# A fused attention, dense and expert kernel: the gather buffer is cleared earlier, `xe` is placed anew, idle products stand in the last routing

## The chip, the cores and the metric

The kernel runs on one core of one Trainium2 chip. The metric is the device time of one execution in microseconds (us). The engines are TensorE (PE in the profile, its weight loads PEld), VectorE (DVE), ScalarE (ACT), GpSimd (POOL) and SyncE (SP, which here only issues DMAs).

## The reference

Three layers follow one another on 1536 tokens (2 batches of 768) of width 512. Shown is the part in which the change lies:

```python
x = attention(q, k, v, lam)                  # linear attention with decay, (1536, 512)
x = (x @ w_a) * (x @ w_b) @ w_out            # dense layer, inner width 1536, float64 weights
# expert layer: 8 experts, 512 -> 1024 -> 512
do_compute = x @ w_skip > 0                  # the other tokens pass through unchanged
logits = xc @ w_gate                         # xc = x[do_compute]
e_idx = np.argmax(logits, axis=1)
gate_w = max(softmax(logits))
y[mask] = gate_w * (relu(xc[mask] @ w1[e]) @ w2[e])     # mask: e_idx == e
out[do_compute] = xc + y
```

## The kernel before

Products of float32 accuracy are made of three products each (`mm3`, line 418): every operand is kept as a high part, written by a ScalarE cast to fp32r, and a low part, the rest, written by VectorE (`lo_part`, line 50). So each stationary or moving operand costs one cast on ScalarE and one subtraction on VectorE before TensorE can use it.

The program goes through these stages, with their places in the profiled execution. Attention (up to 56 us) leaves `xT`. The dense stage (56 to 258 us) runs `phase_a(m, c)` 36 times, 24 products each, and writes the products `a * b` as `g`; SyncE meanwhile loads the next float64 weights, which `conv` turns into `ab` and `wo`. The y stage (258 to 372 us) goes over 12 token tiles of 128 rows: `y_tile(t)` multiplies `g` by `wo` in 12 steps `m` of three products (operands `gs`, from `y_split`), and at each step lets the routing of the tile before go on by one `yield`. That routing, `route`, has the following parts. `logits3` transposes y, cuts it into three bf16 parts `yp` and multiplies them by the gate weights `w9p` (line 605, twelve short products). Then VectorE takes the row maximum `mx`, the index `r`, the one-hot `oh`. `rank` multiplies `oh` by an upper triangle to number the tokens of each expert (`rk`, `rks`), forms the row `key`, and GpSimd scatters the rows of y into the buffer `xs` in DRAM, 128 rows for each of the 8 experts (`place`). Rows of `xs` which nobody writes must read as zero with token number 4096: `clear` writes a zero tile `blank` over all of `xs` at the start of the y stage, by eight SyncE DMAs.

The last tile (11) has a routing of its own, since nothing is left to cover it. Its y is made in two halves of 256 columns, the logits in two halves too (`logits`, lines 577 to 583). Expert 0's rows are not fetched from `xs` as a whole: `px_add` (line 686) adds three products in PSUM, one for `xg0` (the rows placed before tile 10) and two with one-hot matrices `pm` for tiles 10 and 11. From there ScalarE and VectorE make `xe0`.

The expert stage (376 to 477 us) has for each expert: `exp_x` (four transposes `px` of the gathered rows `xg`, then `xe`), `exp_h` twice (12 products `eu,xe` each, then ScalarE's relu into `hr`), `exp_t` (eight transposes of `hr`, then `hT`), and `exp_y` (24 products `eu,hT`, then the gated sum and an indirect DMA to `out`, whose row numbers `ix` are cast from a column of `xg`). The weights `eu` come through six raw buffers `rw` that SyncE fills; `prefetch` says how far ahead loads and casts are written, `load_pair` holds both. At the end stands a loop for tokens beyond 128 in an expert, which is not entered here; its count `npi` comes from `cnt`, `mxc`, `over` and `npf`.

Up to line 463 the order on every engine is that of the code. Behind it a scheduler decides the order on each engine, and each engine works its own queue strictly in order (TensorE can load weights ahead). DMA issues of SyncE also stand in a queue and wait in it for their buffers.

Of the kernel before, what the change touches and what calls it, by code (L numbers as in the profile page):

```python
# [17 lines left out]
P = 128  # L18
# [5 lines left out]
def kernel(ctx, tc, q, k, v, lam, w_a, w_b, w_out, w_skip, w_gate, w1, w2, out):  # L24
# [73 lines left out]
    spin(24)  # L98

# [319 lines left out]

    def phase_a(m, c, work):  # L420
# [12 lines left out]
        for i in range(2):  # L433
            nc.vector.tensor_mul(g[c * 2 + i][m // 4][:, m % 4, :], at[:, i * 256:(i + 1) * 256], pp[1][:, i * 256:(i + 1) * 256])  # L434
# [8 lines left out]
    for m, c in seq:  # L443
        if c == 0 and m + 1 < MT:
            lds, nxt_ab = load_ab(m + 1)
            lds[0]()
            if m < 8 and m % 2 == 0:
                nxt_wo = load_wout(m, W // 2)

        def work():  # L450
            if m == MT - 2:
                steps(nxt_ab, 4 if c == 0 else 0)
            elif m < MT - 2:
                steps(nxt_ab, 2 if c < 2 else 0)
                if c == 2 and m < 8:
                    steps(nxt_wo, 4)
            if (m, c) == (MT - 1, 1):
                steps(load_wout(8), 4)
            if (m, c) == (MT - 2, 2):
                steps(load_wout(10), 4)  # L460

        phase_a(m, c, work)
    msched.close()
# [8 lines left out]
    def load_pair(e, which, j, steady=True):  # L472
        rt = raw.tile([P, 2, W], F32, name=f"rw_{e}_{which}_{j}", tag="raw")
        if which == 0:
            nc.sync.dma_start(out=rt.rearrange("p a b -> p (a b)"), in_=w1[e, j * P:(j + 1) * P, :])
        else:
            nc.sync.dma_start(out=rt, in_=w2[e, j * 2 * P:(j + 1) * 2 * P, :].rearrange("(m p) d -> p m d", p=P))
        n = uno[0]
# [23 lines left out]
    def prefetch(upto):  # L502
        while nxt[0] < min(upto, len(useq)):
            eu[useq[nxt[0]]] = load_pair(*useq[nxt[0]])
            nxt[0] += 1
# [15 lines left out]
    xs = dp.tile([E * P, XW], F32, name="xs")  # L521

    def clear(blank):
        nc.gpsimd.memset(blank[:, :DM + 1], 0.0)  # L524
        nc.gpsimd.memset(blank[:, DM + 1:], 4096.0)
        for e in range(E):
            nc.sync.dma_start(out=xs[e * P:(e + 1) * P, :], in_=blank)

    clear(wk.tile([P, XW], F32, name="blank", tag="y", bufs=3))
# [12 lines left out]
    def y_tile(t, hooks):  # L542
# [3 lines left out]
        nc.gpsimd.iota(yt[:, DM + 1:DM + 2], [[0, 1]], base=t * P, channel_multiplier=1, allow_small_or_imprecise_dtypes=True)  # L546
        for half in range(2 if last else 1):
# [13 lines left out]
            nc.scalar.copy(out=yt[:, cols], in_=py)  # L561
# [8 lines left out]
    def logits(t, yt, lg, k0, k1):  # L570
# [4 lines left out]
        pt = bank([P, n, P], f"yT_{t}_{k0}")  # L575
        for kk in range(k0, k1):
            nc.tensor.transpose(pt[:, kk - k0, :], yt[:, kk * P:(kk + 1) * P], ident)
        yT = wk.tile([P, n, P], F32, name=f"yTs_{t}_{k0}", tag="yT")
        nc.vector.tensor_copy(yT, pt)
# [7 lines left out]
    def logits3(t, yt, lg):  # L587
# [12 lines left out]
        for _ in range(6):  # L600
            yield
# [8 lines left out]
    def route(t, yt, lg=None):  # L610
# [3 lines left out]
        if last:  # L614
            yield from logits(t, yt, lg, 2, KT)
# [14 lines left out]
        nc.vector.reduce_max(out=r, in_=cand, axis=AX)  # L630
        ina = sm("ina", 1)
        nc.vector.tensor_scalar(out=ina, in0=act, scalar1=-FAR, scalar2=FAR + E * P, op0=ALU.mult, op1=ALU.add)
        oh = sm("oh", E, BF16)
        nc.vector.tensor_scalar(out=oh, in0=cand, scalar1=r, scalar2=act, op0=ALU.is_equal, op1=ALU.mult)
# [12 lines left out]
    def rank(t, yt, oh, es):  # L647
# [6 lines left out]
        nc.tensor.matmul(rk, lhsT=upper, rhs=oh, start=(t == 0), stop=True)  # L654
        jk = sm("jk", E)
# [50 lines left out]
    def exp_x(e, xg):  # L706
# [3 lines left out]
        xe = wk.tile([P, 2, KT, P], F32R, name=f"xe_{e}", tag="xe")  # L710
# [60 lines left out]
    prefetch(17)  # L771
    do_h(0)
# [10 lines left out]
    hTs[0] = exp_t(0, hrs[0])  # L783
    for e in range(E):
        prefetch(8 * e + 14)

# [21 lines left out]
    passes = nc.values_load(npi[0:1, 0:1], min_val=0, max_val=NT1 - 1)  # L808
    with tc.For_i(0, passes):
# [10 lines left out]
        for t in range(NT1):  # L820
# [3 lines left out]
            nc.gpsimd.iota(yt[:, DM + 1:], [[0, 1]], base=t * P, channel_multiplier=1, allow_small_or_imprecise_dtypes=True)  # L824
# [33 lines left out]
```

## Time and profile before

| | us |
|---|---|
| three runs | 488.21, 490.44, 491.65 |
| median | 490.44 |
| profiled execution | 488.71 |
| its span in the trace | 486.9 |
| TensorE busy | 467.7 (96%) |
| VectorE busy | 367.8 (76%) |
| ScalarE busy | 219.5 (45%) |

Times in the rows further down count from the start of the span; a row of a timeline joins neighbouring instructions of one kind (its count behind the x) and gives the start of the first and the time to the end of the last. Ends of products are modelled, and products overlap, so a pace is read from starts. In brackets stands the idle time of the engine before the row, and what ended it.

### The profile page before, as it was taken

How to read it: one execution, taken by the hardware profiler on the slowest of the kernel's cores; microseconds unless marked ns; L12 is line 12 of the kernel's file. 1: busy time of each engine (PE TensorE's matmuls, PEld its weight loads, DVE VectorE, ACT ScalarE, POOL GpSimd, SP SyncE). 2: the span in 40 equal slices, each digit the busy share in tenths (PEclk: the TensorE clock that was granted, in tenths of full speed). 3: DMA queues.
4: the chain of work that ended last, by engine and by line, in shares of the span. 5: the costliest groups of instructions: out<-in, count | busy, mean ns of one | idle time of the engine just before them, and what ended most of it. 6: DMA issues, size and time to landing. Idle time of an engine off the chain costs nothing. (4 is left out here: it accounts for less than half of the span.)

```text
span 486.9 us, 7861 instructions
## 1 busy us (share of the span) xinstructions
PE 467.7 (96%) x2874; PEld 386.9 (79%) x2874; DVE 367.8 (76%) x740; ACT 219.5 (45%) x380; POOL 57.9 (12%) x84
## 2 busy tenths in 40 slices
PE   8999899999999999999999899999998999999991
PEld 6788788888888888888888678887788788888881
DVE  6568988888888888675495797776676579899880
ACT  3244333233323332222132754654553569877760
POOL 3544000000000000000000141121122000101000
PEclk9999999999999999999999999999999999999998
DMA  9999531421322314311207950110114898999941
GB/s 174 217 218 217 132 123 51 174 86 50 124 86 87 127 46 149 112 39 47 87 0 191 366 180 34 51 51 36 47 51 144 301 375 290 347 343 365 322 147 41
DMA packets 71629, 73.41 MB, mean 151 GB/s; under 512 B 41510, under 2 KB 53798, under 8 KB 71584
## 3 DMA queue, kind: packets, MB, share of 16 engines
q1 hardware_dynamic: 68880, 66.37, 43.7%
q0 software_dynamic: 2560, 6.47, 3.5%
q8 instruction: 24, 0.39, 0.3%
q14 instruction: 21, 0.17, 0.1%
q10 hardware_dynamic: 144, 0.00, 0.0%
HBM read 64.26 MB, written 10.51 MB: 154 GB/s over the span
## 5 line engine op out<-in xcount | busy, mean ns | idle before, releaser
L418 PE MATMUL psum<-xT,ab 128*128 128x512 f32 x864 | 196.1, 389 | 0.0
L418 PEld LDWEIGHTS psum<-xT,ab 128*128 128x128 f32 x864 | 162.1, 188 | 33.8 <-issue 0.2
L418 PE MATMUL psum<-wo,gs 128*128 128x512 f32 (+1 forms) x468 | 105.4, 378 | 0.0
L418 PEld LDWEIGHTS psum<-wo,gs 128*128 128x128 f32 x468 | 82.0, 188 | 14.6
L50 DVE TENSOR_TENSOR eu<-rw,eu 128x512 fp32r<-128x512 f32 (+1 forms) x92 | 78.5, 896 | 13.2 <-ACT eu L487 8.1
L434 DVE TENSOR_TENSOR g<-at,psum 128x256 f32<-128x256 f32 x72 | 27.0, 418 | 35.5 <-PE psum L418 35.5
L432 ACT COPY at<-psum 128x512 f32<-128x512 f32 x36 | 21.0, 585 | 61.0 <-PE psum L418 57.2
L418 PE MATMUL psum<-eu,xe 128*128 128x512 f32 x192 | 47.7, 405 | 0.0
L418 PE MATMUL psum<-eu,hT 128*128 128x512 f32 x192 | 47.2, 395 | 0.0
L538 ACT CAST gs<-g 128x256 fp32r<-128x256 f32 x78 | 31.4, 405 | 31.1 <-PE psum L418 24.7
L418 PEld LDWEIGHTS psum<-eu,xe 128*128 128x128 f32 x192 | 37.2, 194 | 8.9 <-ACT xe L696 0.2
L50 DVE TENSOR_TENSOR gs<-g,gs 128x256 fp32r<-128x256 f32 x78 | 32.7, 422 | 12.4 <-ACT gs L538 11.7
L418 PEld LDWEIGHTS psum<-eu,hT 128*128 128x128 f32 x192 | 35.4, 188 | 7.3
L487 ACT CAST eu<-rw 128x1024 fp32r<-128x1024 f32 x36 | 36.8, 1053 | 3.3 <-DMA rw<-in_moe_w 3.1
L483 ACT CAST eu<-rw 128x512 fp32r<-128x512 f32 x56 | 31.4, 628 | 3.6 <-DVE gs L50 3.6
L524 POOL MEMSET blank<- 128x513 f32 x1 | 0.5, 530 | 209.4 <-PE psum L418 209.4
L118 ACT CAST wo<-tt_wo 128x512 fp32r<-128x512 f32 (+1 forms) x10 | 7.1, 709 | 31.7 <-DVE tt_wo L115 31.7
L754 POOL DMA_INDIRECT out<-xg,ix x8 | 10.0, 1253 | 92.0 <-DVE xg L753 62.2
L118 ACT CAST ab<-tt_ab 128x1024 fp32r<-128x1024 f32 (+1 forms) x13 | 12.8, 986 | 14.4 <-DVE tt_ab L115 14.4
L111 ACT ACTIVATE sg_ab<-ab_r 128x1024 f32<-128x1024 f32 (+1 forms) x13 | 13.9, 1067 | 11.5 <-DVE wo L122 11.3
L532 POOL DMA_INDIRECT xs<-y,key x12 | 15.5, 1292 | 24.8 <-DVE key L665 11.3
L219 ACT COPY kT<-psum 128x1024 f32<-128x1024 f32 (+1 forms) x7 | 6.3, 894 | 21.9 <-PE psum L210 21.9
(133 smaller groups left out, 528.3 us busy)
## 6 DMA issues: line engine op xcount, KB each, us to landing
rw<-in_moe_w SPq DMA_DIRECT2D x64, 512.0 KB, 5.8
wo_r<-in_moe_w_out SPq DMA_DIRECT2D x12, 512.0 KB, 3.7
ab_r<-in_moe_w_a SPq DMA_DIRECT2D x11, 512.0 KB, 3.6
ab_r<-in_moe_w_b SPq DMA_DIRECT2D x11, 512.0 KB, 4.7
vr<-in_v SPq DMA_DIRECT2D x12, 256.0 KB, 5.1
out<-y POOLq DMA_DIRECT2D x12, 256.0 KB, 2.5
xg<-xs SPq DMA_DIRECT2D x9, 257.0 KB, 5.6
xs<-blank SPq DMA_DIRECT2D x8, 257.0 KB, 5.0
```

Source lines behind the costliest of these rows:

```text
L50: nc.vector.tensor_sub(dst, src, hi.bitcast(F32))
L111: nc.scalar.activation(out=sf, in_=Hw.bitcast(F32), func=AF.Abs)
L118: nc.scalar.copy(out=hi, in_=tf)
L219: nc.scalar.copy(out=tT[:, cs], in_=pt[:, cs])
L418: nc.tensor.matmul(out_, lhsT=ls[a], rhs=rs[b_], start=first and n == 0, stop=last and n == 2)
L432: nc.scalar.copy(out=at, in_=pp[0])
L434: nc.vector.tensor_mul(g[c * 2 + i][m // 4][:, m % 4, :], at[:, i * 256:(i + 1) * 256], pp[1][:, i * 256:(i + 1) * 256])
L483: nc.scalar.copy(out=u[:, 0], in_=rt[:, i])
L487: nc.scalar.copy(out=pu[:, :, 0], in_=rt)
L532: nc.gpsimd.indirect_dma_start(out=xs, out_offset=bass.IndirectOffsetOnAxis(ap=key, axis=0), in_=yt, in_offset=None, bounds_check=E * P - ...
L538: nc.scalar.copy(out=gs[:, 0], in_=src)
L754: nc.gpsimd.indirect_dma_start(out=out, out_offset=bass.IndirectOffsetOnAxis(ap=ix, axis=0), in_=xg[:, :DM], in_offset=None, bounds_check= ...
```

## The change

It has seven parts.

1. The buffer `xs` is cleared in the dense stage: after `phase_a(m, 2)` of the first eight `m`, SyncE writes zeros over the 512 data columns of one expert's rows from the small tile `zero`, and the last two columns from a tile `nobody`. The eight `xs<-blank` DMAs at the start of the y stage go. The token number is now kept as an integer, so that `exp_y` uses the column of `xg` as it is, without the cast `ix`.
2. In the y stage, `prefetch(..., later=True)` issues the raw load of a weight and leaves its casts to the next tile's turn.
3. The logits product of tile 0 comes nine steps behind its transposes in place of six.
4. Idle products of zeros (128x256, bf16, into a PSUM tile that is no longer read) stand in the last routing: one ahead of the rank product, five behind it, three ahead of expert 0's first product. The count product moves behind expert 0's `exp_h`.
5. The second half of tile 11's y, and its transposed copy `yTs`, are each copied by ScalarE and VectorE, 128 columns each.
6. From the last routing to the start of expert 0 TensorE and VectorE follow the order of the code, TensorE on to the end of expert 0. So on VectorE `pm` now comes right behind the rank sum `rks`; before, a reciprocal and the row maximum `mxc` stood between them.
7. `xe` gets a pool of its own, which moves it from byte 352 to byte 480 of a 512-byte line in the built program; the weights `eu`, `hT`, `gs` and `xe0` stand at 480 in both kernels. The read of `npi` stands two experts earlier.

On ScalarE, at the start of the y stage, the casts of the first expert weights (`eu<-rw`) stand between those of tiles 0 and 1 (`gs`, `y`, `yp`). Before:

```order
L538 CAST gs_10_2262<-g_2_852 128x256
L538 CAST gs_0_2280<-g_0_850 128x256
L538 CAST gs_2_2302<-g_0_850 128x256
L561 COPY y_2215<-psum 128x512
L538 CAST gs_4_2311<-g_1_851 128x256
L538 CAST gs_6_2320<-g_1_851 128x256
L596 CAST yp_0_2294<-psum 128x512
L487 CAST eu_2275<-rw_0_0_2273 128x2x512
L598 CAST yp_0_2295<-yr_2297 128x512
```

Now:

```order
L565 CAST gs_10_2270<-g_2_852 128x256
L515 CAST eu_2385<-rw_0_0_2281 128x2x512
L565 CAST gs_0_2285<-g_0_850 128x256
L515 CAST eu_2507<-rw_0_1_2388 128x2x512
L565 CAST gs_2_2307<-g_0_850 128x256
L592 COPY y_2223<-psum 128x512
L565 CAST gs_4_2316<-g_1_851 128x256
L515 CAST eu_2630<-rw_0_2_2510 128x2x512
L565 CAST gs_6_2325<-g_1_851 128x256
L633 CAST yp_0_2299<-psum 128x512
```

The first weight cast has moved from behind tile 0's `yp` to ahead of tile 1's `gs_0`, and the next ones follow between the `gs` of that tile.

On TensorE, in the last routing, from the logits of the second half row to expert 0's first products (`xe_3762` and `xe_3783` are `xe0`). Before:

```order
L686 MATMUL psum<-pm_2212,y_3386 128x128
L583 MATMUL psum<-w_156,yTs_2_3711 128x9 x2
L686 MATMUL psum<-pm_2212,y_3386 128x128
L653 LDWEIGHTS ones
L653 MATMUL psum<-ohs,ones 128x8
L654 LDWEIGHTS upper
L654 MATMUL psum<-oh_3733,upper 128x8
L774 LDWEIGHTS ones
L774 MATMUL psum<-ohs,ones 128x8
L686 MATMUL psum<-pm_2213,y_3512 128x128 x4
L418 MATMUL psum<-eu_2275,xe_3762 128x512 x3
```

Now, where L104 are idle products (five pairs stand at the first "LDWEIGHTS zero" behind L696, three behind `y_3514`; the others read alike):

```order
L620 MATMUL psum<-w_156,yTs_2_3724 128x9 x2
L730 MATMUL psum<-pm_2220,y_3394 128x128 x4
L104 LDWEIGHTS zero
L104 MATMUL psum<-zero 128x256
L695 LDWEIGHTS ones
L695 MATMUL psum<-ohs,ones 128x8
L696 LDWEIGHTS upper
L696 MATMUL psum<-oh_3744,upper 128x8
L104 LDWEIGHTS zero
L104 MATMUL psum<-zero 128x256
```

The products with `pm` of tile 10 stand together behind the logits, an idle product stands ahead of the rank, and the idle ones have taken the place of the count product (L774).

On TensorE, in the second half of expert 0 (L735 and L783 transpose `hr`, L709 and L757 the gathered rows `xg`). Before:

```order
L735 MATMUL psum<-ident,hr_3823 128x128 x4
L709 MATMUL psum<-ident,xg_3777 128x128 x2
L735 MATMUL psum<-ident,hr_3823 128x128 x4
L418 MATMUL psum<-eu_2750,hT_0_3771 128x512 x2
L709 MATMUL psum<-ident,xg_3777 128x128 x2
L709 MATMUL psum<-ident,xg_3779 128x128
L418 MATMUL psum<-eu_2750,hT_0_3771 128x512
L418 MATMUL psum<-eu_2751,hT_0_3771 128x512 x3
L418 MATMUL psum<-eu_2758,hT_0_3771 128x512 x3
L418 MATMUL psum<-eu_2759,hT_0_3771 128x512 x3
L709 MATMUL psum<-ident,xg_3779 128x128 x3
L418 MATMUL psum<-eu_2766,hT_1_3772 128x512 x3
```

Now:

```order
L822 LDWEIGHTS ones
L822 MATMUL psum<-ohs,ones 128x8
L783 MATMUL psum<-ident,hr_3850 128x128 x8
L424 MATMUL psum<-eu_2880,hT_0_3796 128x512 x3
L424 MATMUL psum<-eu_2881,hT_0_3796 128x512 x3
L424 MATMUL psum<-eu_2886,hT_0_3796 128x512 x3
L424 MATMUL psum<-eu_2887,hT_0_3796 128x512 x3
L757 MATMUL psum<-ident,xg_3802 128x128 x4
L757 MATMUL psum<-ident,xg_3804 128x128 x4
L424 MATMUL psum<-eu_2892,hT_1_3797 128x512 x3
```

The transposes of `xg`, which stood in ones, twos and threes among the others, now stand in one block behind `hT_0`'s products.

The diff, without the parts on the overflow loop and on moved declarations:

```diff
+    def idle(n):
+        for _ in range(n):
+            nc.tensor.matmul(idle_to[0], lhsT=wz[:, :P], rhs=wz, start=True, stop=True)
...
+    nobody = wat.tile([P, XW - DM], F32, name="nobody", bufs=1)
+    nc.gpsimd.memset(nobody[:, :1], 0.0)
+    nc.gpsimd.memset(nobody.bitcast(I32)[:, 1:], 4096)
+
+    def clear_first(e):
+        nc.sync.dma_start(out=xs[e * P:(e + 1) * P, :DM].rearrange("p (a b) -> p a b", b=P), in_=zero.rearrange("p (a b) -> p a b", a=1).to_broadcast([P, DM // P, P]))
+        nc.sync.dma_start(out=xs[e * P:(e + 1) * P, DM:], in_=nobody)
...
         phase_a(m, c, work)
+        if c == 2 and m < E:
+            clear_first(m)
...
-    def prefetch(upto):
+    held = []
+
+    def prefetch(upto, later=False):
+        for n, rt in held:
+            eu[useq[n]] = load_pair(*useq[n], rt=rt)
+        held.clear()
         while nxt[0] < min(upto, len(useq)):
-            eu[useq[nxt[0]]] = load_pair(*useq[nxt[0]])
+            if later:
+                held.append((nxt[0], load_raw(*useq[nxt[0]])))
+            else:
+                eu[useq[nxt[0]]] = load_pair(*useq[nxt[0]])
             nxt[0] += 1
...
-    clear(wk.tile([P, XW], F32, name="blank", tag="y", bufs=3))
...
-            nc.scalar.copy(out=yt[:, cols], in_=py)
+            if half:
+                nc.scalar.copy(out=yt[:, 2 * P:3 * P], in_=py[:, :P])
+                nc.vector.tensor_copy(yt[:, 3 * P:4 * P], py[:, P:])
+            else:
+                nc.scalar.copy(out=yt[:, cols], in_=py)
...
-        nc.vector.tensor_copy(yT, pt)
+        if k0:
+            nc.scalar.copy(out=yT[:, 0], in_=pt[:, 0])
+            nc.vector.tensor_copy(yT[:, 1], pt[:, 1])
+        else:
+            nc.vector.tensor_copy(yT, pt)
...
-        for _ in range(6):
+        for _ in range(6 if t else 9):
             yield
...
+            px_add(0, xg0, ident, True, False)
+            last_logits = logits(t, yt, lg, 2, KT)
+            next(last_logits)
+            next(last_logits)
+            px_add(1, xg0, ident, True, False)
+            yield from last_logits
             for i in range(2):
-                px_add(i, xg0, ident, True, False)
                 px_add(i, yts[t - 1], pms[t - 1], False, False)
+            idle(1)
...
+        if last:
+            idle(5)
...
-        prefetch(([1, 2, 3, 4] + [4 + (3 * (i // 2 + 1) // 2) for i in range(2, 10)])[t])
+        prefetch(([1, 2, 3, 4] + [4 + (3 * (i // 2 + 1) // 2) for i in range(2, 10)])[t], t < NT1 - 1)
+    msched.enter_context(tc.manual_schedule(engines={mybir.EngineType.PE, mybir.EngineType.DVE}))
     for _ in hooks:
         pass
+    idle(3)
...
+    msched.close()
     hctx.close()
+    xep = ctx.enter_context(tc.tile_pool(name="xe", bufs=2))
...
-        xe = wk.tile([P, 2, KT, P], F32R, name=f"xe_{e}", tag="xe")
+        xe = xep.tile([P, 2, KT, P], F32R, name=f"xe_{e}", tag="xe")
...
-        ix = wk.tile([P, 1], I32, name=f"ix_{e}", tag="ix", bufs=8)
-        nc.vector.tensor_copy(ix, xg[:, DM + 1:DM + 2])
+        ix = xg.bitcast(I32)[:, DM + 1:DM + 2]
...
+    msched.enter_context(tc.manual_schedule(engines={mybir.EngineType.PE}))
     do_h(0)
...
+        if e == 1:
+            msched.close()
+        if e == E - 2:
+            passes = nc.values_load(npi[0:1, 0:1], min_val=0, max_val=NT1 - 1)
```

## Rows read from the trace of the kernel before

**Rows 1.** Page, part 1: busy time of an engine (share of the span), its instructions.

```profile
PE 467.7 (96%) x2874; PEld 386.9 (79%) x2874; DVE 367.8 (76%) x740; ACT 219.5 (45%) x380; POOL 57.9 (12%) x84
```

**Rows 2.** Timeline of TensorE at tile 0's logits: start us, us, engine, line, operation, count [idle before].

```profile
271.90 0.19 PE L605 MATMUL psum<-w9p,yp 128*128 128x27 bf16 x1
272.65 0.19 PE L605 MATMUL psum<-w9p,yp 128*128 128x27 bf16 x1 [0.56 <-ACT yp L598]
273.99 0.41 PE L605 MATMUL psum<-w9p,yp 128*128 128x27 bf16 x10 [1.16 <-DVE yp L599]
274.26 0.94 PE L418 MATMUL psum<-wo,gs 128*128 128x512 f32 x3
```

**Rows 3.** Timeline of TensorE at the same burst of tile 1.

```profile
283.08 0.46 PE L605 MATMUL psum<-w9p,yp 128*128 128x27 bf16 x12
283.39 2.98 PE L418 MATMUL psum<-wo,gs 128*128 128x512 f32 x12
```

**Rows 4.** Timelines at the start of the y stage: TensorE, then ScalarE.

```profile
257.81 9.69 PE L418 MATMUL psum<-wo,gs 128*128 128x512 f32 x42
...
263.45 0.41 ACT L538 CAST gs<-g 128x256 fp32r<-128x256 f32 x1 [0.95 <-PE psum L418]
...
271.03 1.05 ACT L487 CAST eu<-rw 128x1024 fp32r<-128x1024 f32 x1 [2.47 <-DMA rw<-in_moe_w]
```

**Rows 5.** Timeline of SyncE's DMA queue at the start of the y stage.

```profile
258.77 4.68 SPq L527 DMA_DIRECT2D xs<-blank  x8
263.57 2.26 SPq L475 DMA_DIRECT2D rw<-in_moe_w  x4
```

**Rows 6.** Tile `rw`, 256 to 285: from issue to landing of its loads.

```profile
DMA to landing us min/median/max: 3.5/7.4/9.9
```

**Rows 7.** Timeline of the last routing, all engines.

```profile
371.58 0.42 DVE L579 COPY yTs<-psum 128x256 f32<-128x256 f32 x1 [2.86 <-PE psum L577]
...
373.79 0.17 PE L654 MATMUL psum<-oh,upper 128*128 128x8 bf16 x1 [0.79 <-DVE ek L635]
...
374.26 0.17 DVE L776 TENSOR_REDUCE mxc<-psum 128x1 f32<-128x8 f32 x1
374.34 0.34 DVE L658 TENSOR_SCALAR pm<-siota,rks,ek 128x128 f32<-128x128 f32 x1
...
374.73 1.16 PE L686 MATMUL psum<-pm,y 128*128 128x128 f32 x8 [0.51 <-DVE far L663]
```

**Rows 8.** Windows: busy time (count) of each engine, granted clock, DMA share, GB/s.

```profile
372.00:376.00 4.00, 2.59 (x20) 2.04 (x19) 2.65 (x23) 0.75 (x4) 0.18 (x1) 1.00 0.19 70
376.00:380.00 4.00, 4.00 (x11) 3.15 (x12) 1.96 (x3) 1.24 (x2) 0.81 (x1) 0.57 0.24 56
440.00:460.00 20.00, 20.00 (x101) 16.72 (x100) 17.49 (x22) 16.18 (x23) 1.71 (x1) 1.00 0.98 354
```

**Rows 9.** Timeline of TensorE at the start of the program.

```profile
1.14 4.27 PE L96 MATMUL psum<-zero 128*128 128x256 bf16 x24 [1.14 <-DVE warm L153]
```

**Rows 10.** Timeline of TensorE in the expert stage.

```profile
375.90 7.34 PE L418 MATMUL psum<-eu,xe 128*128 128x512 f32 x24
...
409.59 5.75 PE L418 MATMUL psum<-eu,xe 128*128 128x512 f32 x24
415.18 2.90 PE L418 MATMUL psum<-eu,hT 128*128 128x512 f32 x12
417.92 0.60 PE L709 MATMUL psum<-ident,xg 128*128 128x128 f32 x4
```

**Rows 11.** Timeline of TensorE in the second half of expert 0.

```profile
383.52 0.38 PE L709 MATMUL psum<-ident,xg 128*128 128x128 f32 x2
383.94 0.65 PE L735 MATMUL psum<-ident,hr 128*128 128x128 f32 x4
...
384.98 0.49 PE L709 MATMUL psum<-ident,xg 128*128 128x128 f32 x3
385.23 2.56 PE L418 MATMUL psum<-eu,hT 128*128 128x512 f32 x10
```

More of the change, by code (lines that the diff above doesn't have):

```diff
@@ L98 @@
     spin(24)
+    idle_to = []
+    def idle(n):
+        for _ in range(n):
+            nc.tensor.matmul(idle_to[0], lhsT=wz[:, :P], rhs=wz, start=True, stop=True)
     tiny = 1.125 * 2.0 ** -15
@@ L418, in mm3, with clear @@
             nc.tensor.matmul(out_, lhsT=ls[a], rhs=rs[b_], start=first and n == 0, stop=last and n == 2)
+    xs = dp.tile([E * P, XW], F32, name="xs")
+    def clear(blank):
+        nc.gpsimd.memset(blank[:, :DM + 1], 0.0)
+        nc.gpsimd.memset(blank.bitcast(I32)[:, DM + 1:], 4096)
+        for e in range(E):
+            nc.sync.dma_start(out=xs[e * P:(e + 1) * P, :], in_=blank)
+    nobody = wat.tile([P, XW - DM], F32, name="nobody", bufs=1)
[4 more added lines that the diff above has]
+        nc.sync.dma_start(out=xs[e * P:(e + 1) * P, DM:], in_=nobody)
     def phase_a(m, c, work):
@@ L470, with load_raw @@
     uno = [0]
-    def load_pair(e, which, j, steady=True):
+    def load_raw(e, which, j):
         rt = raw.tile([P, 2, W], F32, name=f"rw_{e}_{which}_{j}", tag="raw")
@@ L477, in load_pair @@
             nc.sync.dma_start(out=rt, in_=w2[e, j * 2 * P:(j + 1) * 2 * P, :].rearrange("(m p) d -> p m d", p=P))
+        return rt
+    def load_pair(e, which, j, steady=True, rt=None):
+        rt = load_raw(e, which, j) if rt is None else rt
         n = uno[0]
@@ L520 @@
     ohs = cp.tile([P, E], BF16, name="ohs")
[L521 to L527, printed above, removed]
-    clear(wk.tile([P, XW], F32, name="blank", tag="y", bufs=3))
     def place(yt, key):
@@ L545, in y_tile @@
         yts[t] = yt
-        nc.gpsimd.iota(yt[:, DM + 1:DM + 2], [[0, 1]], base=t * P, channel_multiplier=1, allow_small_or_imprecise_dtypes=True)
+        nc.gpsimd.iota(yt.bitcast(I32)[:, DM + 1:DM + 2], [[0, 1]], base=t * P, channel_multiplier=1)
         for half in range(2 if last else 1):
@@ L575, in logits @@
         pt = bank([P, n, P], f"yT_{t}_{k0}")
+        if not k0:
+            idle_to.append(pt)
         for kk in range(k0, k1):
@@ L614, in route @@
         if last:
-            yield from logits(t, yt, lg, 2, KT)
             pxs.extend(bank([P, 2, P], f"px0_{i}") for i in range(2))
+            px_add(0, xg0, ident, True, False)
[4 more added lines that the diff above has]
+            yield from last_logits
             for i in range(2):
-                px_add(i, xg0, ident, True, False)
                 px_add(i, yts[t - 1], pms[t - 1], False, False)
+            idle(1)
         else:
@@ L630, in route @@
         nc.vector.reduce_max(out=r, in_=cand, axis=AX)
+        oh = sm("oh", E, BF16)
+        nc.vector.tensor_scalar(out=oh, in0=cand, scalar1=r, scalar2=act, op0=ALU.is_equal, op1=ALU.mult)
         ina = sm("ina", 1)
         nc.vector.tensor_scalar(out=ina, in0=act, scalar1=-FAR, scalar2=FAR + E * P, op0=ALU.mult, op1=ALU.add)
-        oh = sm("oh", E, BF16)
-        nc.vector.tensor_scalar(out=oh, in0=cand, scalar1=r, scalar2=act, op0=ALU.is_equal, op1=ALU.mult)
         nc.vector.scalar_tensor_tensor(out=ek[:, col], in0=r, scalar=-float(P), in1=ina, op0=ALU.mult, op1=ALU.add)
@@ L783 @@
     hTs[0] = exp_t(0, hrs[0])
+    passes = None
     for e in range(E):
         prefetch(8 * e + 14)
+        if e == 1:
+            msched.close()
+        if e == E - 2:
+            passes = nc.values_load(npi[0:1, 0:1], min_val=0, max_val=NT1 - 1)
         def hook():
@@ L806 @@
             do_h(e + 2)
-    passes = nc.values_load(npi[0:1, 0:1], min_val=0, max_val=NT1 - 1)
     with tc.For_i(0, passes):
@@ L823 @@
             nc.vector.tensor_copy(yt[:, DM:DM + 1], gts[:, t:t + 1])
-            nc.gpsimd.iota(yt[:, DM + 1:], [[0, 1]], base=t * P, channel_multiplier=1, allow_small_or_imprecise_dtypes=True)
+            nc.gpsimd.iota(yt.bitcast(I32)[:, DM + 1:], [[0, 1]], base=t * P, channel_multiplier=1)
             place(yt, ki[:, t:t + 1])
```

## The prediction

> **What bounds the kernel now.** I read the page first: TensorE is busy for 96% of the span [rows 1], so the time is the sum of TensorE's own work, plus the few places where it stands still or runs slowly, and an edit elsewhere counts only through those. The second view is TensorE's timeline, searched for idle gaps; the third the granted clock by stretch; the fourth the pace of equal products with different operands. They give four places.
>
> First, tile 0 of the y stage. The logits product of line 605 should be a burst of twelve between two blocks of `wo,gs`. It starts at 271.90, and the next `wo,gs` only at 274.26: 2.36 us, with two gaps [rows 2]. In a later tile the same burst goes from 283.08 to 283.39, 0.31 us [rows 3]. So **2.05 us** are lost. The second operand of the burst, `yp`, is cast by ScalarE, and in front of that cast in ScalarE's queue stands the cast of the first expert weight, which waited 2.47 us for its DMA until 271.03 [rows 4]. SyncE issued that load at 263.57, behind eight writes `xs<-blank` that began at 258.77 [rows 5]; seven such loads took a median of 7.4 us to land, the best 3.5 [rows 6].
>
> Second, the last routing: a chain of small operations between TensorE and VectorE, in which TensorE has idle gaps of 0.79 and 0.51 us [rows 7]. [...] Fourth, the pace in the experts: 24 products on `xe` go from 409.59 to 415.18, 5.59 us, and the 12 on `hT` from 415.18 to 417.92, 2.74 [rows 10]. Twice 2.74 is 5.48, so `xe` costs 0.11 us more per expert.
>
> **The change part by part.** The sum is made against the profiled execution, 488.71 us (486.9 of span and 1.8 around it).
>
> *Clearing in the dense stage, raw loads ahead of their casts, logits three steps later.* The eight `xs<-blank` writes leave the front of the weight loads, so that SyncE can issue the first load where it issued the first blank, about 258.8, and with a landing of 3.5 to 7.4 us it is there by 262.3 to 266.2, in place of 271.0. The casts move too: the order shows the first one behind `gs_10` and before `gs_0` of tile 1, no longer in front of `yp`'s second part. Then nothing that waits for DMA is queued ahead of `yp`, and three more steps (nine products at 0.23 us, about 2.1 us) lie between the transposes and the burst. I take the whole stall away: **-2.05**. At worst 1 us of it comes back, because the routing of tile 0 now starts 2 us later and its one-hot must still be there when TensorE reaches the rank product; at best nothing more is to be had. The sixteen new SyncE writes cost nothing by my count: by the eight blanks (4.68 us of SyncE for eight [rows 5]) a pair takes about 1.2 us of SyncE in one of eight dense blocks of 24 products (5.5 us), in which weight loads are issued well ahead. If that cover is too thin, a late `ab` load would stop TensorE by up to that 1.2 us, once. VectorE loses eight casts of `ix`, and the overflow count moves into expert 0; neither is on the path.
>
> *Last routing.* Nine idle products are added. [...] `pm` now follows the rank directly, without the reciprocal and the row maximum of 374.26 (0.17 us) [rows 7] between: -0.15. The copies of the last half row are split over ScalarE and VectorE. Were they to run together, half of each of the two copies would go (a copy of 256 columns takes 0.42 [rows 7]): -0.4. But both halves lie in one PSUM bank, and the order with its waits shows VectorE's half waiting for ScalarE's. Then the two run in turn, each with its own fixed price, at about +0.1 to +0.2 for both places together. I take the second: the routing as a whole **0.0**, bounds -0.5 and +0.4.
>
> [...]
>
> *The clock.* The idle products and the denser order fill the stretch before 376. With them TensorE's busy time in 372 to 376 rises from 2.59 [rows 8] by about 1 us. The drop came behind the only stretch of this kind, and not behind the tile-0 stall, which is shorter. I take it as gone: **-1.7**. Whether nine products are enough, no row shows; that is a rival.
>
> *Expert 0 in program order.* Before, the transposes of the next gathers filled waits: two at 383.52, before the second half of `hr` came at 383.94, and three at 384.98, before the low part of `hT` [rows 11]. The new order puts all eight in one block behind `hT_0`. The five transposes (0.25 + 0.25 us) then stand for themselves, and TensorE waits in their place: **+0.5**, between 0 and +0.7.
>
> *`xe` modulo 512 bytes.* In the built program the weights, `hT` and `gs` lie at 480 modulo 512, `xe` at 352 before and 480 after. If that is what makes `xe` slower than `hT`, 7 experts x 0.11 = **-0.8**; the other end is 0.
>
> [...]
>
> *Weights.* The expert stage would go about 2 us faster (1.7 + 0.8 - 0.5), while the DMA engines are 0.98 busy in 440 to 460 with TensorE never idle [rows 8]. The stream starts earlier too, since its buffers come free with the earlier y stage, but it cannot go much faster. I charge **+0.4**, between 0 and +1.5.
>
> Sum: -2.05 + 0.0 - 1.7 + 0.5 - 0.8 + 0.4 = -3.65, so 485.1 for the profiled execution. The median of the three runs before is 490.44, 1.7 above its profiled one; what the other runs had more no trace tells. I take half of that, 0.9, with the forecast: **486.0 us**.
>
> **The rivals.** *The clock drops all the same*, in the routing or just behind it. For it: the added work is a fraction of a microsecond in each gap, and the transposes and 9-column products around it are as light as before. Price 1.7: 487.7. *The weights become the bound.* For it: 0.98 of DMA share; against it: TensorE has no idle time there now. All of the 2 us that the stage gains, less the 0.4 charged, would reappear as waits near 450 to 461: +1.5, 487.5. [...]
>
> *The weight casts stop the y stage*, the one that ends slower. In the new order ScalarE's cast of the first weight stands in front of `gs_0` of tile 1, which ScalarE now casts at 263.45 [rows 4]. TensorE needs it when 36 of the 42 products from 257.81 are done [rows 4], 257.81 + 36 x 0.23 = 266.1. Ahead of that lie `gs_0`'s cast (0.41), its low part (about 0.4) and the weight's cast (1.05): the load must have landed by 264.1. Every microsecond beyond is a wait of TensorE; at 271.0, where it landed before, 6.9, which gives 486.0 + 6.9 = 492.9, slower than now. It decides at 264.1. A landing of 3.5 from 258.8 is 1.8 us ahead of it; at the median of 7.4, which was measured behind the blanks, 2.1 us would be lost: 488.1. *The gain is larger*: the copies do run side by side, weights keep up, and the slower runs before had further clock drops that go too: -0.8 to -2.5, around 484.3.
>
> **How the numbers follow.** Chances: forecast 0.40, clock drops 0.18, weights 0.10, placement 0.14, casts stop the y stage 0.06, larger gain 0.12. A measurement of this kernel tells about 1% from no change, here 4.9 us: below 485.5 is faster, above 495.3 slower. Of the forecast's runs a good 0.4 would fall below 485.5, of the clock, weight and placement rivals 0.25, of the larger gain all: 0.17 + 0.10 + 0.12 = 0.39. Slower by over 1% is the worse half of the casts' rival: 0.03. The range takes in both ends of the single terms and all rivals but the casts' worse half: 482.8 to 489.0.
>
> **What would show it.** The profile of the changed kernel should show the tile-0 burst at 0.31 us without a gap, the first weight cast near 263 and no `gs` late behind it; the granted clock at 1.00 in the stretch of expert 0's first 24 products, and these in about 5.7 us; two short gaps beside `hr` and `hT` in expert 0; 24 products on `xe` in 5.48 us from start to start; and at most one short wait for a weight late in the expert stage. Wrong would be the prediction if a gap of a microsecond appeared before `gs_0` of tile 1, or a clock below 1.00 behind the routing.

## The result, and the profile after

The changed kernel took 484.18 us (median of four runs, 484.02 to 484.69), the kernel before 489.32 beside it (488.13 to 491.65): a ratio of 0.989, with a 95% interval from 0.985 to 0.993. Its profiled execution took 484.69 us, with a span of 482.8; before it was 488.71 and 486.9. Repeated in another set of runs, the changed kernel took 484.37 and the kernel before 487.46 (ratio 0.9935, 0.992 to 0.995).

TensorE's timeline of the changed kernel at tile 0's logits (L642 is the burst that was L605):

```profile
273.94 0.46 PE L642 MATMUL psum<-w9p,yp 128*128 128x27 bf16 x12
274.25 2.30 PE L424 MATMUL psum<-wo,gs 128*128 128x512 f32 x9
...
281.34 3.88 PE L424 MATMUL psum<-wo,gs 128*128 128x512 f32 x16
```

The burst starts 2.04 us later than before (273.94 against 271.90 [rows 2], the time of nine products) and stands without a gap: 0.31 us from 273.94 to 274.25. The next products after tile 1's burst start at 281.34, 2.05 us earlier than before [rows 3]; the stall of [rows 2] is gone as a whole. ScalarE's timeline of the changed kernel shows why:

```profile
263.38 1.05 ACT L515 CAST eu<-rw 128x1024 fp32r<-128x1024 f32 x1 [0.89 <-DMA rw<-in_moe_w]
264.34 0.40 ACT L565 CAST gs<-g 128x256 fp32r<-128x256 f32 x1
```

The first weight cast starts at 263.38, when its load has landed, and not at 271.03 [rows 4]. ScalarE stands idle for it for 0.89 us, but `gs_0` of tile 1 follows at 264.34 and TensorE is not held up by it. Weight casts still stand ahead of the second part of `yp` in ScalarE's queue, four of them by the trace, but only this first one waited for its load, and it waited early enough.

The last routing of the changed kernel, all engines (L104 are the idle products, L589 and L590 the copies of y, L613 and L614 those of `yTs`):

```profile
368.44 0.39 PE L730 MATMUL psum<-ident,xg 128*128 128x128 f32 x2
368.64 0.27 ACT L589 COPY y<-psum 128x128 f32<-128x128 f32 x1 [2.41 <-PE psum L424]
...
368.99 0.29 DVE L590 COPY y<-psum 128x128 f32<-128x128 f32 x1 [2.31 <-ACT y L589]
...
369.70 0.27 ACT L613 COPY yTs<-psum 128x128 f32<-128x128 f32 x1 [0.80 <-PE psum L610]
370.00 0.29 DVE L614 COPY yTs<-psum 128x128 f32<-128x128 f32 x1 [0.72 <-ACT yTs L613]
...
371.80 0.71 PE L104 MATMUL psum<-zero 128*128 128x256 bf16 x5
...
372.62 1.16 PE L730 MATMUL psum<-pm,y 128*128 128x128 f32 x8
...
373.89 5.69 PE L424 MATMUL psum<-eu,xe 128*128 128x512 f32 x24
```

VectorE's half of y starts when ScalarE's is over (368.64 + 0.27 = 368.91), and so again at 369.70 and 370.00: the halves run in turn. From the two products on `xg` at 368.44 to expert 0's first product at 373.89 are 5.45 us. The idle products run at about 0.1 us each (0.71 us for the five, of which 0.27 are the last one's own) and end before `pm` is ready, at 372.51 against 372.62. In the next lines (columns as in [rows 8]) the first is the kernel before's, from its last products on `xg` ahead of y's transposes to expert 0's first product; the second is the same stretch of the changed kernel; the third, also of the changed kernel, lies behind it, where the granted clock is 1.00:

```profile
370.48:375.90 5.42, 4.01 (x33) 3.46 (x31) 2.97 (x23) 1.05 (x4) 0.67 (x2) 1.00 0.19 69
```

```profile
368.44:373.89 5.45, 5.15 (x42) 4.24 (x40) 3.08 (x20) 1.27 (x6) 0.58 (x1) 1.00 0.18 67
376.00:380.00 4.00, 4.00 (x21) 3.06 (x19) 1.70 (x3) 1.92 (x3) 0.00 (x0) 1.00 0.54 172
```

TensorE's busy time in the routing rose from 4.01 to 5.15 us, and the granted clock from 376 to 380 from 0.57 to 1.00 [rows 8]. (The window from 372 to 376 of [rows 8] can't be set beside the changed kernel, whose routing stands 2 us earlier.) Expert 0's first 24 products take 5.53 us, from 373.89 to the next block at 379.42; before they took 7.18, from 375.90 to 383.08. These are the places of the kernel before at which its stages end:

```profile
370.48 0.39 PE L686 MATMUL psum<-ident,xg 128*128 128x128 f32 x2
...
383.08 0.60 PE L735 MATMUL psum<-ident,hr 128*128 128x128 f32 x4
...
390.72 8.53 PE L418 MATMUL psum<-eu,xe 128*128 128x512 f32 x36
```

TensorE in the expert stage of the changed kernel:

```profile
379.42 0.18 PE L822 MATMUL psum<-ohs,ones 128*128 128x8 bf16 x1
...
380.26 0.66 PE L783 MATMUL psum<-ident,hr 128*128 128x128 f32 x4 [0.17 <-ACT hr L772]
...
383.88 1.03 PE L757 MATMUL psum<-ident,xg 128*128 128x128 f32 x8
...
387.53 8.32 PE L424 MATMUL psum<-eu,xe 128*128 128x512 f32 x36
...
406.13 5.60 PE L424 MATMUL psum<-eu,xe 128*128 128x512 f32 x24
411.57 2.88 PE L424 MATMUL psum<-eu,hT 128*128 128x512 f32 x12
```

The eight transposes of `xg` (383.88) stand in one block, and TensorE waits where they had filled in, as at 380.26. The 24 products on `xe` go from 406.13 to 411.57, 5.44 us, against 5.59 before [rows 10].

With these places the two spans can be subtracted stage by stage (the last 36 products start at 468.33 before and at 464.04 in the changed kernel):

| stretch of TensorE | before | after | difference |
|---|---|---|---|
| y stage, to the `xg` products of the last routing | up to 370.48 | up to 368.44 | -2.04 |
| last routing, to expert 0's first product | 5.42 | 5.45 | +0.03 |
| expert 0's first 24 products, to the next block | 7.18 | 5.53 | -1.65 |
| second half of expert 0, to the next `xe` products (now with the count product at 379.42) | 7.64 | 8.11 | +0.47 |
| from there to the last 36 products | 77.61 | 76.51 | -1.10 |
| last 36 products and the end | 18.57 | 18.76 | +0.19 |
| span | 486.9 | 482.8 | -4.1 |

The +0.19 of the last stretch is not explained; in another profile of the changed kernel (e6) it takes 18.59.

### The profile page after: what moved, and what is told of

It is laid out like the page before. It is cut to its first block, busy times and chain, and to the rows that moved or that the text cites. A ratio compares the mean times of both kernels' runs of the same rounds, so it can differ in the third digit from the quotient of the medians.

```text
span 482.8 us, 7882 instructions
## 1 busy us (share of the span) xinstructions
PE 466.7 (97%) x2883; PEld 386.7 (80%) x2883; DVE 368.0 (76%) x733; ACT 220.0 (46%) x381; POOL 57.5 (12%) x84
## 5 line engine op out<-in xcount | busy, mean ns | idle before, releaser
L424 PE MATMUL psum<-eu,xe 128*128 128x512 f32 x192 | 45.0, 390 | 0.0
L424 PEld LDWEIGHTS psum<-eu,xe 128*128 128x128 f32 x192 | 35.9, 188 | 7.4
L573 POOL IOTA y<- 128x1 int32 x12 | 1.4, 124 | 211.1 <-PE psum L424 197.4
L801 POOL DMA_INDIRECT out<-xg x8 | 12.9, 1617 | 86.5 <-DVE xg L800 34.9
L121 DVE SCALAR_TENSOR_TENSOR tt_ab<-sg_ab,tt_ab 128x1024 f32<-128x1024 f32 (+1 forms) x13 | 14.9, 1143 | 1.2
```

The lines of the kernel that those rows point to most:

```text
L121: nc.vector.scalar_tensor_tensor(out=tf, in0=sf, scalar=tiny, in1=tf, op0=ALU.is_ge, op1=ALU.mult)
L424: nc.tensor.matmul(out_, lhsT=ls[a], rhs=rs[b_], start=first and n == 0, stop=last and n == 2)
L801: nc.gpsimd.indirect_dma_start(out=out, out_offset=bass.IndirectOffsetOnAxis(ap=ix, axis=0), in_=xg[:, :DM], in_offset=None, bounds_check= ...
```

## The experiments

Times of one set of runs are compared with the kernel before in the same set, since its median was 489.3 in one and 487.1 to 487.7 in three others.

**The idle products left out (e1_no_idle).**

```diff
     def idle(n):
-        for _ in range(n):
+        for _ in range(0):
```

> The changed kernel without its nine idle products; all else stays. Theory (the idle products keep the clock): behind the last routing a stretch at half speed comes back, about 3.4 us long, expert 0's first 24 products take about 7.2 us in place of 5.52, and the time is 1.7 us above the changed kernel's 484.2, about 485.9. Rival (the denser order of the last routing alone keeps the clock): granted clock 1.00 throughout, 5.5 us for these products, 484.2 or up to 0.1 less, since nothing is issued in vain.

It took 484.45 us (484.10 to 486.17); the kernel before 487.13; ratio 0.995 (0.9935 to 0.996). The window over the routing and the first half of expert 0 in the kernel before, the same window in this run, this run's routing alone (368.86 to 374.32), and two places of its TensorE timeline:

```profile
370.00:384.00 14.00, 12.55 (x68) 10.29 (x67) 6.54 (x29) 4.61 (x10) 1.57 (x2) 0.88 0.40 138
```

```profile
370.00:384.00 14.00, 12.68 (x70) 9.91 (x69) 7.43 (x28) 5.56 (x12) 1.57 (x2) 1.00 0.48 153
368.86:374.32 5.46, 4.44 (x33) 3.53 (x31) 3.09 (x20) 1.28 (x6) 0.58 (x1) 1.00 0.18 65
```

```profile
374.32 5.73 PE L424 MATMUL psum<-eu,xe 128*128 128x512 f32 x24
379.89 0.18 PE L822 MATMUL psum<-ohs,ones 128*128 128x8 bf16 x1
...
455.88 2.57 PE L424 MATMUL psum<-eu,xe 128*128 128x512 f32 x10
458.79 3.49 PE L424 MATMUL psum<-eu,xe 128*128 128x512 f32 x14 [0.34 <-DVE eu L50]
```

The clock stayed at 1.00 and the 24 products took 5.57 us: the rival holds. Its six runs had mean clocks of 0.992 to 0.995, where 14 of the 24 runs of the kernel before beside it had 0.991 or less. Its slowest run, the profiled one, is slow for other reasons. The last two rows show one: TensorE waited for a weight's low part behind ten products on `xe`, and went on at 458.79 in place of 458.15. It also waited 0.3 us for a low part of `hT` at 382.28, and its dense stage began 0.4 us later than the changed kernel's.

**`xe` back at 352 (e2_xe_352), and two more places (e11_xe_224, e12_xe_96).** The unused room is 96, 64 and 32 floats:

```diff
+    xpad = ctx.enter_context(tc.tile_pool(name="xpad", bufs=1))
+    xpad.tile([P, 96], F32, name="xpad")
     xep = ctx.enter_context(tc.tile_pool(name="xe", bufs=2))
```

> The changed kernel with 384 bytes of unused room ahead of xe, so that xe stands at 352 modulo 512 again; nothing else moves. Theory (the place modulo 512 sets the pace of products on xe): 24 of them take 5.59 us from start to start in place of 5.44, seven times 0.15, so 1.1 us slower than the changed kernel, about 485.2. [...]

> The changed kernel with 256 bytes of unused room ahead of xe, which stands at 224 modulo 512; the weights stay at 480. Theory (what counts is the same place modulo 512): 24 products on xe in about 5.59 us, as at 352. Rival (a shorter period of 256 bytes counts): 5.44 us, as at 480.

> The changed kernel with 128 bytes of unused room ahead of xe, which stands at 96 modulo 512. Theory (any place but that of the weights is slow): 5.59 us. Rival (only some distances cost): something between 5.44 and 5.59, and different from that at 224.

TensorE's timeline at 24 products on `xe`, first at 352, then at 224, then at 96:

```profile
406.86 5.75 PE L424 MATMUL psum<-eu,xe 128*128 128x512 f32 x24
412.45 2.90 PE L424 MATMUL psum<-eu,hT 128*128 128x512 f32 x12
```

```profile
406.56 5.60 PE L424 MATMUL psum<-eu,xe 128*128 128x512 f32 x24
412.00 2.89 PE L424 MATMUL psum<-eu,hT 128*128 128x512 f32 x12
```

```profile
406.16 5.75 PE L424 MATMUL psum<-eu,xe 128*128 128x512 f32 x24
411.75 2.90 PE L424 MATMUL psum<-eu,hT 128*128 128x512 f32 x12
```

From start to start: 5.59, 5.44, 5.59 us. At 352 the time was 485.51 (485.09 to 486.02), 1.1 above the 484.37 of the changed kernel in the next set (the kernel before: 487.13 and 487.46), and 1.06 above e1's 484.45 in its own set, as the theory has it. The kernels at 224 and 96 ran once each, in 485.00 and 485.53 us; from the second expert's first products to the last 36 of the stage they take 76.54 and 77.62 us, where the changed kernel takes 76.51. So 224 is as fast as 480. Places 256 bytes apart took the same: 5.44 at 480 and 224, 5.59 at 352 and 96. Of the expectation for 224 the rival holds. The room moves the tiles behind `xe` (`xg`, `hr`) along with it, against the expectation's "nothing else moves"; the 24 products read neither.

**The kernel before with `xe` at 480 (e3_b_xe480).**

```diff
+    xep = ctx.enter_context(tc.tile_pool(name="xe", bufs=2))
     wk = ctx.enter_context(tc.tile_pool(name="wkE", bufs=2))
...
-        xe = wk.tile([P, 2, KT, P], F32R, name=f"xe_{e}", tag="xe")
+        xe = xep.tile([P, 2, KT, P], F32R, name=f"xe_{e}", tag="xe")
```

> The kernel before with xe in a pool of its own, at 480 modulo 512, and nothing else changed. Theory (the place sets the pace): 24 products on xe in 5.44 us in place of 5.59, 1.1 us faster than the kernel before in the profiled spans (486.9 to 485.8), if the weights keep up. Rival (the place does nothing): 5.59 us, 486.9.

```profile
409.04 5.60 PE L418 MATMUL psum<-eu,xe 128*128 128x512 f32 x24
414.48 2.89 PE L418 MATMUL psum<-eu,hT 128*128 128x512 f32 x12
```

These rows of its TensorE timeline give 5.44 us again, and from the second expert's first products to the last 36 are 76.48 us against 77.61 before: 1.13 less, as the theory has it, with the weights keeping up. The time was 486.31 (484.55 to 487.20) against 487.13, ratio 0.998 (0.9965 to 0.9988): 0.8 us faster.

**The clearing alone (e4_b_clear).** The kernel before, with `clear_first` in the dense stage as in the change's diff and without `clear` in the y stage.

> The kernel before with the clearing of xs moved to the dense stage and nothing else: no later casts, six steps ahead of tile 0's logits. Theory (the loads behind the blanks were the cause, and the three further steps hide what is left): the first weight cast starts near 263.4, and tile 0's logits burst, at 271.9, waits about 0.4 us for the third part of yp, which in the changed kernel ended at 272.27; so 1.6 of the 2.05 us are won, span 485.3. Rival (the later casts or the steps are needed): a wait of 1 us or more at 271.9 remains, span 486 or more.

TensorE's timeline at tile 0's logits (L613 here):

```profile
272.28 0.21 PE L613 MATMUL psum<-w9p,yp 128*128 128x27 bf16 x2
272.34 0.71 PE L418 MATMUL psum<-wo,gs 128*128 128x512 f32 x2
272.90 0.41 PE L613 MATMUL psum<-w9p,yp 128*128 128x27 bf16 x10
273.16 3.89 PE L418 MATMUL psum<-wo,gs 128*128 128x512 f32 x16
```

The scheduler put two products between those of the burst, and only 0.1 us is lost: 0.88 from 272.28 to 273.16, of which two products are 0.46 and the burst 0.31. From the first `wo,gs` product to the last `xg` products ahead of y's transposes e4 takes 110.76 us (258.19 to 368.95), against 112.67 before and 110.63 in the changed kernel. So the clearing alone takes the stall away. The first weight cast already stands ahead of tile 1's `gs_0` here, at 263.83, so the later casts are not what moved it. But the time was 486.53 against 487.13 (ratio 0.9987, 0.998 to 0.9997): 0.6 us, less than the 1.6 of the theory. A part of the difference stands in expert 0's second half, which takes 8.30 us here (381.43 to 389.73) against 7.64 before. VectorE, then TensorE:

```profile
383.39 0.15 DVE L752 CAST ix<-xg 128x1 int32<-128x1 f32 x1 [1.51 <-DMA xg<-xs]
```

```profile
384.20 2.59 PE L418 MATMUL psum<-eu,hT 128*128 128x512 f32 x10 [0.39 <-DVE hT L50]
```

With TensorE earlier, VectorE's cast `ix` of a later expert waits for that expert's gather, the low part of `hT` stands behind it, and TensorE waits for the low part. The changed kernel has no such cast. Another part of the difference is the size of the stall in the kernel before, which a second profile shows.

**The kernel before, once more (e5_before_again).** No edit.

> The kernel before, unchanged, for a second profile, since its median differed by 2 us between two sets of runs (489.32 and 487.13). Theory (the stall at tile 0 is as long as the weight load behind the blanks takes to land): here the load lands before 271.0, the first weight cast starts near 270, and the gap at tile 0's logits is about 1 us in place of 2.05. Rival (the difference lies elsewhere, in the clock or the dense stage): the gap is again 2 us and another stage is shorter.

Its ScalarE timeline at the first weight cast, and TensorE's at the burst:

```profile
269.87 1.05 ACT L487 CAST eu<-rw 128x1024 fp32r<-128x1024 f32 x1 [1.51 <-DMA rw<-in_moe_w]
```

```profile
271.71 0.21 PE L605 MATMUL psum<-w9p,yp 128*128 128x27 bf16 x2
...
273.10 4.33 PE L418 MATMUL psum<-wo,gs 128*128 128x512 f32 x18
```

The load had landed at 269.87, 1.2 us earlier than in the first profile, and the stall is 273.10 - 271.71 - 0.31 = 1.08 us in place of 2.05. Its stretch of lower granted clock behind the routing was there again (0.88 over 370 to 384, as in the first profile). So the stall's size goes with the landing of that load. In e3 the same sum gives 0.92, and in e8 1.2; in e3 a further 0.8 us is lost at tile 1's transposes (278.24), which wait for a copy of y that stands behind weight casts on ScalarE, and there the second weight's load was late as well.

**The changed kernel, once more (e6_after_again).** No edit.

> The changed kernel, unchanged, beside the others of this set. Theory (no half-speed stretch behind its last routing): none of its runs has a mean clock of 0.991 or below, where 14 of 24 runs of the kernel before had it, and its runs stand within 0.7 us of each other. Rival: some runs have it, and are about 1 us longer.

It took 484.37 us (484.21 to 484.71), with mean clocks of 0.993 to 0.995 and a clock of 1.00 over 370 to 384: the theory holds. Of the 14 runs of the kernel before beside it ten had a mean clock of 0.991 or less; that bound alone doesn't find them all, since e5 had the stretch at a mean of 0.992.

**Expert 0 left to the scheduler (e7_sched0).**

```diff
-    msched.enter_context(tc.manual_schedule(engines={mybir.EngineType.PE}))
     do_h(0)
...
-        if e == 1:
-            msched.close()
```

> The changed kernel with expert 0 left to the scheduler, which puts the transposes of xg back in ones, twos and threes among those of hr and the products on hT; the order of the last routing stays. Theory (the block order costs 0.5): from expert 0's first transposes of hr to the next products on xe 7.6 us in place of 8.1, and 0.4 to 0.5 us faster than the changed kernel. Rival (the time is lost elsewhere, weights or a wait in the next expert): the same time as the changed kernel.

TensorE's timeline in expert 0 (L757 are the transposes of `xg`, L783 those of `hr`):

```profile
379.56 0.63 PE L783 MATMUL psum<-ident,hr 128*128 128x128 f32 x4
380.24 0.44 PE L757 MATMUL psum<-ident,xg 128*128 128x128 f32 x2
...
381.44 0.49 PE L757 MATMUL psum<-ident,xg 128*128 128x128 f32 x3
...
387.17 8.33 PE L424 MATMUL psum<-eu,xe 128*128 128x512 f32 x36
```

The transposes are back in the waits, and from the count product just ahead of these rows, at 379.52, to 387.17 are 7.65 us, against 8.11 in the changed kernel (379.42 to 387.53). The time was 484.20 (483.22 to 484.99) beside 484.37 for the changed kernel: the 0.46 us are seen in the trace, but not settled by the times.

**The idle products alone, in the kernel before (e8_b_idle).** `idle(1)`, `idle(5)` and `idle(3)` at the same places of the code as in the change.

> The kernel before with the nine idle products alone; the scheduler puts eight of them ahead of the rank product, so the gap behind it stays. Theory (idle products alone keep the clock up): no run with a mean clock of 0.991 or below, about 1 us faster in the runs which had it. Rival (the order of the last routing does it, as the changed kernel without idle products suggests, or neither is needed): about half of the runs still have it, and the time stays within 0.3 us of the kernel before.

It took 485.95 us (485.52 to 486.42) against 487.46, ratio 0.997 (0.996 to 0.998). None of its nine runs had a mean clock below 0.992, and its first 24 products took 5.59 us. All nine idle products stand ahead of the rank product, and the gap of 0.51 us behind it stayed. Its window and its routing alone (columns as above):

```profile
370.00:384.00 14.00, 13.18 (x81) 10.92 (x80) 8.42 (x32) 5.77 (x11) 1.58 (x2) 1.00 0.48 162
369.31:374.74 5.43, 4.86 (x43) 4.28 (x41) 2.94 (x23) 1.05 (x4) 0.74 (x2) 1.00 0.21 75
```

Here the theory holds: the idle products alone keep the clock up in the order of before, too.

**Whole copies (e9_whole_copies), and whole copies with expert 0 left to the scheduler (e10_whole_sched).**

```diff
-            if half:
-                nc.scalar.copy(out=yt[:, 2 * P:3 * P], in_=py[:, :P])
-                nc.vector.tensor_copy(yt[:, 3 * P:4 * P], py[:, P:])
-            else:
-                nc.scalar.copy(out=yt[:, cols], in_=py)
+            nc.scalar.copy(out=yt[:, cols], in_=py)
...
-        if k0:
-            nc.scalar.copy(out=yT[:, 0], in_=pt[:, 0])
-            nc.vector.tensor_copy(yT[:, 1], pt[:, 1])
-        else:
-            nc.vector.tensor_copy(yT, pt)
+        nc.vector.tensor_copy(yT, pt)
```

Compared is the stretch from the last `xg` products ahead of y's transposes to expert 0's first product, 5.45 us in the changed kernel.

> The changed kernel with the copies of the last half row as before: y by ScalarE alone, its transposed copy by VectorE alone. [...] Rival (the second engine's copy overlaps the transpose of the first half, so that nothing is lost): 5.45, within 0.1.

> The changed kernel with whole copies and with expert 0 left to the scheduler. Theory (both parts cost, and their prices add): 0.5 from expert 0 and 0.3 from the routing, about 0.8 us faster than the changed kernel, 483.5. Rival (the expert stage is bound by the weights by now, and gives the lead back): a wait of TensorE for a weight late in the expert stage, and 484.0 or more.

The timeline of the routing in e9, all engines, and of its TensorE behind expert 0:

```profile
368.40 0.39 PE L722 MATMUL psum<-ident,xg 128*128 128x128 f32 x2
368.60 0.37 ACT L588 COPY y<-psum 128x256 f32<-128x256 f32 x1 [2.41 <-PE psum L424]
...
369.50 0.42 DVE L608 COPY yTs<-psum 128x256 f32<-128x256 f32 x1 [2.85 <-PE psum L606]
```

```profile
373.75 5.73 PE L424 MATMUL psum<-eu,xe 128*128 128x512 f32 x24
...
388.76 7.57 PE L424 MATMUL psum<-eu,xe 128*128 128x512 f32 x32 [0.65 <-DVE xe L50]
```

The whole copies take 0.37 and 0.42 us, and the routing 373.75 - 368.40 = 5.35: 0.10 shorter than with the split, at the edge of the rival's 0.1. It is small but steady: the seven profiled kernels with the split take 5.45 or 5.46 there, the two without 5.34 and 5.35. The split costs a little and brings nothing. The time was 484.26 (483.81 to 485.60) against 487.73; the profiled run lost 0.8 us at 388.76, where `xe`'s low part came late (two products on it had started at 387.48): on VectorE it stands behind two low parts of weights, and ScalarE had stood idle for 3.04 us until the load of the first of them landed. e10 took 483.98 (483.02 to 484.21) against 487.73, ratio 0.992 (0.990 to 0.993). Its routing took 5.34 and the second half of expert 0 7.66, so its trace has both gains, 0.6 us together, and TensorE waited for no weight late in the stage. Beside the changed kernel's 484.37 from another set that is 0.4, less than the 0.8 expected (0.3 of it for the routing, an estimate of the author's; the trace shows 0.11), and within what the sets differ by. It is the fastest version here; that it beats the changed kernel is read from the stages, not proved by the times.

## Why the prediction was right, step by step

The forecast was 486.0 with a range of 482.8 to 489.0, and 484.18 was measured. The sum for the profiled execution was 485.1, against 484.69. The gain was put at 4.4 us from the median of 490.44; it was 5.1 in the first set of runs, 3.1 in the next, and 4.0 between the two profiled executions.

- **The stall at tile 0, -2.05:** -2.04 in the profile. The cause was right, and e4 shows it apart: the clearing alone makes the y stage 1.91 us shorter. The later casts and the three further steps were not needed for that; alone they were not run. The reading that nothing which waits for DMA is queued ahead of `yp` was not right: weight casts still are, and it is the earlier landing that made them harmless. What was not seen is that the stall has no fixed size (1.08 in e5, 0.92 at the burst in e3), so its price differs. Between the two profiles of the kernel before (488.71 and 487.28 us) it makes 0.97 of the 1.43; that it is also why the kernel before stood at 489.3 in one set and 487.5 in another, beside a changed kernel at 484.2 and 484.4, is likely, but no trace shows it.
- **Put at nothing:** the sixteen writes did cost nothing, since the dense stage takes 195.97 us from its first product to the first of the y stage in both kernels. The casts of `ix`, "not on the path", are not so harmless: that holds in the kernel before, but in e4, where TensorE came earlier, one of them stood in the way, for about 0.66 us. So removing them belongs to what makes the earlier clearing pay.
- **The last routing, 0.0:** +0.03. The copies do run in turn, at 0.10 more than whole ones; the rest of the routing thus gained 0.07, less than the 0.15 put down for `pm`, which was not run apart. The rows name ScalarE's copy as what VectorE's half waited for (368.99 behind 368.91). That the bank is the reason was not shown: both halves also go into one tile. Of the idle products, 24 took 4.27 us at the program's start, 0.18 each [rows 9], and in the routing one takes 0.1; the granted clock was 1.00 in both places (1 to 5 us in the kernel before, 370 to 384 in the changed one), and why those at the start took longer no run shows.
- **The clock, -1.7:** -1.65. The term can be read from [rows 8]: 4.00 us at a granted clock of 0.57 lose 4.00 x 0.43 = 1.7. The effect was right, its reason only half so: the term took idle products and new order together, and each suffices without the other (e8, e1). The four profiled kernels with the old order of the routing and no idle products (before, e3, e4, e5) all had a stretch of lower granted clock, 0.88 over 370 to 384 (0.50 from 377 to 379 in the first profile); the ten others had 1.00 there. One such profile alone would prove little, since not all runs of the old order have low mean clocks: 31 of the 47 runs of the kernel before beside the experiments had 0.991 or less. But of the 50 runs of the ten other kernels none had. In the routing TensorE was busy for 4.01 to 4.12 us in the four, 4.44 in e1, 4.86 in e8 and 5.15 in the changed kernel (1.14 more than before, about the 1 us that was put down), so the clock was kept where TensorE stood still less. Whether that decides, or the kind and order of the products, is open. The price in the median is less sure than in the profile: among the 24 runs of the kernel before beside e1, those with a mean clock above 0.991 were 0.7 us faster in the mean (486.7 against 487.4), among e3's twelve 1.3 (485.3 against 486.6).
- **Expert 0 in program order, +0.5:** +0.47, and e7 gives 0.46 back.
- **`xe`, -0.8:** -1.1 by the stages; the term was too small, because 24 products on `hT` were taken as the goal (5.48), while `xe` reached 5.44. That the place does it is shown by e2 and e3 from both sides: 0.15 us for 24 products, 6 ns for each. So the case of a placement without effect (chance 0.14, 0.8 us more) did not come.
- **The weights, +0.4:** 0.0 in the profile, where TensorE waits for none. The price was not baseless: TensorE waits for a weight in e1 (458.79), and for an `xe` behind late weights in e2 (388.37) and e9 (388.76), with idle times of 0.25 to 0.65 us in single runs.
- **From the profiled run to the median, +0.9:** this was the largest error, 1.4 us, since the changed kernel's median lies 0.5 below its profiled run. The changed kernel's runs lie within 0.7 us, those of the kernel before within 1.6 to 3.5, according to the set; that the stall's size and the clock make this scatter fits the traces, but most of these runs have none.

The measured time lies 1.8 us below the forecast, next to the rival of a larger gain (around 484.3, chance 0.12). Of that rival's three reasons one holds, that the weights keep up; the copies do not run side by side, and what clock drops the slower runs had is not shown. So the median came out near that rival's number without its mechanism, while the profile followed the forecast's sum term by term, with `xe` and the weights 0.3 and 0.4 better than put down.

The rival by which the weight casts stop the y stage had its deciding point at 264.1 for the landing of the first load. It landed by 263.38, 0.7 us on the safe side, and by 263.40 in e6: that rival was closer than its 0.06 suggests.

## What to carry to other kernels

A stall whose length is the landing time of one DMA should be priced as a range (here 2.05 us with the cast behind the load at 271.03, 1.08 with it at 269.87) and looked for in the scatter of the runs: with its cause removed the runs here also came closer together (within 0.7 us, before within 1.6 to 3.5). Work that is off the path stays off it only as long as the engine that waits for it comes no earlier: `ix` cost nothing before, and 0.66 us in e4. Where a stretch of short products follows a long busy one, look at the granted clock behind it (0.57 here from 376 to 380), not only at the gaps; nine products of zeros, about 0.1 us each, held it here at 1.00 in the old order (e8), while in the new order it stood at 1.00 without them (e1). And before an operand is blamed for its pace, compare equal products with another operand from start to start: 0.15 us in 5.6 was real, and came back by moving the tile.

## What the runs showed that was not expected

- The pace of the products on `xe`, their 128x128 weight operand, changed with its place: 24 of them took 5.44 us with `xe` at 480 or 224 modulo 512 and 5.59 with it at 352 or 96, the moving operand standing at 480 each time. No other places were tried. Whether the distance to the moving operand counts, or the place alone, no run here tells.
- Nine products of zeros, about 1 us in all, or else a new order of the same work, made the difference between 7.18 us and 5.59 (e8) or 5.57 (e1) for the 24 products behind them; with both it was 5.53.
- Copies of 128 columns by ScalarE (0.27) and VectorE (0.29) cost 0.56 together in turn, against 0.37 (ScalarE) or 0.42 (VectorE) for one of 256: by an estimate from these two sizes, some 0.16 of each copy is a fixed price.
